# Attention and two gated layers in one kernel: five plain chunks and two units by seven products in the first layer, and attention placed every 13.5 gaps

## The chip, the cores and the metric

The kernel runs on one core of one Trainium2 chip. The metric is the device time of one execution in microseconds (us), the median of several. The engines of the core work side by side, each through its own list of instructions in program order: TensorE (PE in the profile, with its weight loads as PEld), VectorE (DVE), ScalarE (ACT), GpSimd (POOL) and SyncE (SP), which here issues nearly all transfers.

## The reference

Three stages, each fed by the one before, for 8 x 576 = 4608 tokens of 512 features.

```
kv  = einsum('bhsd,bhse->bhde', k, v)            # 8 batches, 8 heads, 576 tokens, 64 features
o   = einsum('bhsd,bhde->bhse', q, kv)
x   = o / sqrt(mean(o * o, -1) + 1e-6) * g_norm   # then laid out as 4608 x 512
x2  = ((x @ w1) * (x @ w2)) @ w3 @ w_out          # 512 -> 1024, 1024 -> 1024 -> 512
h   = x2 @ moe2_w_in                              # 512 -> 2048
out = (h * sigmoid(h)) @ moe2_w_out               # 2048 -> 512
```

All arrays are float32.

## The kernel before

**Precision.** Every large product runs in three passes: an operand is split into a high part (a cast to fp32r on ScalarE, `split`, L108) and a low part (a subtraction on VectorE), and TensorE adds high x high, high x low and low x high (`passes`, L112). Weights arrive as 64-bit words and are made into float32 on the chip by two ScalarE activations and one VectorE operation (`cv_scale`, `cv_bits`).

**Opening.** The list `ORDER` (L59) is written out by hand. It loads and splits w3 and the first layer's output weights, multiplies them into one matrix (`wch`, `wcl`), and computes attention for the first chunk of 512 tokens.

**First phase, plain chunks** (L791 to L844). There are nine chunks of 512 tokens. Those in `PLAIN` (L30: seven, all but 4 and 8) go through the first layer here. A chunk is 8 steps, and a step is three groups of 12 matmuls of 512 columns: `pa` and `pb` (the two input products) and, for the step before, the product with the combined matrix (`g2_mm`). Between the groups ScalarE copies `pa`, VectorE multiplies, and the result is split for the next step's third group. After the eighth step four output tiles are copied out of PSUM and written to DRAM (`x2d`).

Two other kinds of work are threaded between the groups:

- *Attention* of chunks 1 to 8. `event` (L664) puts each of its parts at a place counted in gaps; a gap is one group of 12 matmuls, and places are kept in half gaps. `att_step` (L694) emits what is due. For each chunk: k and v are loaded (`kv_load`, tiles 0 to 2 and later 3 and 4) and multiplied (`kv_mm`), the result is copied (`kv_out`); q is loaded (`q_load`, four tiles); two halves of `att_a` (TensorE) and `att_b` (four ScalarE operations); `att_c`, the row sums of squares on TensorE (L389); `att_d`, three ScalarE operations (L397 to L399); `att_e`, two VectorE operations; `att_h`, a ScalarE cast; `att_l`, a VectorE operation (L417); two halves of `att_r`, the matmuls that spread the scales (L427), and `att_x`, the VectorE products; and `att_f`, which splits the chunk into `xh`, `xl`, or, for a chunk that is not plain (`LATER`), writes it to DRAM (`xd`). The products of attention use two PSUM banks in turn. Chunk c + 1 is placed 20 gaps after chunk c (13 for the last).
- *Weights for the last phase* (`pieces`). `advance` (L295) takes the list one piece further: it writes the blocks that are ready to DRAM (`flush`), asks SP for the raw words three pieces ahead, and casts, scales, joins, sums and subtracts. The last phase needs each weight block in seven forms (the block's quarters and sums of them), each split. Sixteen blocks come from DRAM in three pieces each (`block`), twelve from weights that are on the chip already (`sum`). `ensure` calls `advance` twice a step, after the `pa` group and after the `pb` group.

**Last phase, seven products** (from L994). Units of `UNITS` (L32) hold twice as many tokens as the width given there. A unit is a list of blocks, and a block multiplies a 2 x 2 arrangement of quarters with seven products in place of eight; each product is 2 x 2 x 3 = 12 matmuls (`run`, L865). A unit "A" puts 1024 tokens that attention left in `xd` through the first layer in six blocks (a, b, a, b, out, out); a unit "B" puts tokens through the second layer in eight. Before a block, GpSimd forms sums of the operands (`sums`), and ScalarE and VectorE split them (`step`). After each product ScalarE copies or VectorE adds the result out of PSUM (classes `First`, `Second`, `Silu`, `Out`). The weights of each product (512 KB) are loaded by SP six products ahead in the stream, into the buffer that the product just run has left (`w_load`). The first block of a unit runs before the last block of the unit before.

## Time and profile before

| what | value |
|---|---|
| median of 3 runs | 1402.18 us (1401.04 to 1402.23) |
| the profiled execution, its own time | 1402.33 us |
| its span, first to last instruction | 1400.2 us |
| mean granted TensorE clock (share of 2.4 GHz) | 0.999 |
| busy share of PE, DVE, ACT, POOL | 99%, 59%, 46%, 21% |
| moved by DMA | 320.04 MB, mean 229 GB/s |

A busy share is an average over the whole span. What an engine costs is read from what TensorE waits for in each stage: the chain of waits tells that for the whole span, the time line for a few microseconds, and the table of stretches gives the busy time of each engine in a stage.

### The profile page before, as it was taken

Reading aid. Unit: us, or ns where it says so; the run is one execution under the profiler, and the core shown is the slowest. Engines: PE = TensorE matmul, PEld = TensorE weight load, DVE = VectorE, ACT = ScalarE, POOL = GpSimd, SP = SyncE. Lnnn points to the kernel's source line nnn. Section 1 sums busy time; section 2 is a strip of 40 time slices with the busy share of each in tenths; the row PEclk is TensorE's granted clock in tenths of the full one; section 3 lists DMA queues with packets and bytes.
Section 4 is the critical chain, followed back from the end, with each engine's and each line's share of the span. In section 5 each row is a group of like instructions: output and inputs, shape, how many; then the busy total and the mean of one; then the engine's idle time right before and its main releaser. Section 6 shows DMA issues by size and latency. Waiting matters only on the chain.

```text
span 1400.2 us, 19103 instructions
## 1 busy us (share of the span) xinstructions
PE 1386.7 (99%) x7084; PEld 1152.3 (82%) x7084; DVE 825.4 (59%) x1192; ACT 646.3 (46%) x1019; POOL 291.4 (21%) x190
## 2 busy tenths in 40 slices
PE   7999999999999999999999999999999999999998
PEld 4777787777877778888888888888888889999998
DVE  5856546464656663343764577455854576567458
ACT  5675535444453662323534354543534453543543
POOL 1000000000000002003522435124522352245222
PEclk9999999999999999999999999999999999999999
DMA  9754676769685747076687666866686668888886
GB/s 360 285 181 134 213 240 236 254 202 305 198 265 189 262 163 274 31 254 195 192 259 246 194 193 217 293 194 191 191 299 194 193 209 292 284 255 273 279 254 200
DMA packets 149868, 320.04 MB, mean 229 GB/s; under 512 B 14224, under 2 KB 72592, under 8 KB 149776
## 3 DMA queue, kind: packets, MB, share of 16 engines
q1 hardware_dynamic: 149200, 317.78, 69.3%
q8 instruction: 56, 0.92, 0.3%
q10 hardware_dynamic: 576, 1.05, 0.2%
q14 instruction: 36, 0.29, 0.1%
HBM read 246.42 MB, written 72.35 MB: 228 GB/s over the span
## 4 chain that ended last, share of the span: by engine, by line
PE 96%; DMA 2%; DVE 1%; ACT 0%; SPq 0%; issue 0%
PE ps L878 57%; PE x2ps L114 4%; PE pb L114 4%; PE pa L114 4%; PE x2ps L116 4%; PE x2ps L115 4%; PE pb L116 4%; PE pb L115 4%; PE pa L116 4%; PE pa L115 4%; PE wps L558 2%; PE kvps L338 1%; PE o L370 1%; DMA v<-v_l 1%; PE s L389 1%; DMA more_xl<-wo_l 1%
## 5 line engine op out<-in xcount | busy, mean ns | idle before, releaser
L878 PE MATMUL ps<-xo,w 128*128 128x512 f32 (+1 forms) x2016 | 424.6, 371 | 0.0
L878 PEld LDWEIGHTS ps<-xo,w 128*128 128x128 f32 x2016 | 369.0, 188 | 52.4
L878 PE MATMUL ps<-go,w 128*128 128x512 f32 (+1 forms) x1848 | 387.0, 369 | 0.4 <-issue 0.4
L878 PEld LDWEIGHTS ps<-go,w 128*128 128x128 f32 x1848 | 337.3, 188 | 46.7 <-issue 1.0
L778 DVE TENSOR_TENSOR go<-g,go 128x1024 fp32r<-128x1024 f32 (+1 forms) x110 | 124.9, 1137 | 113.7 <-ACT go L777 112.4
L888 DVE TENSOR_TENSOR c<-ps,c 128x512 f32<-128x512 f32 (+1 forms) x260 | 158.0, 636 | 55.1 <-PE ps L878 53.7
L765 POOL TENSOR_TENSOR x_t<-x2r 128x1024 f32<-128x1024 f32 (+1 forms) x12 | 26.9, 2239 | 543.8 <-DMA x2r<-xd 543.3
L777 ACT CAST go<-g 128x1024 fp32r<-128x1024 f32 (+1 forms) x110 | 104.8, 972 | 46.3 <-PE ps L878 45.1
L815 DVE TENSOR_TENSOR asb<-pb,asb 128x512 f32<-128x512 f32 x56 | 38.6, 690 | 125.4 <-PE pb L116 118.7
L765 POOL TENSOR_TENSOR g_t<-g 128x1024 f32<-128x1024 f32 (+1 forms) x44 | 100.7, 2290 | 49.2 <-DVE g L960 44.4
L765 POOL TENSOR_TENSOR g<-g,g_t 128x1024 f32<-128x1024 f32 (+1 forms) x22 | 48.4, 2198 | 261.4 <-DVE go L778 261.4
L109 ACT CAST ch<-asb 128x512 fp32r<-128x512 f32 x56 | 35.0, 624 | 118.9 <-DVE asb L815 118.7
L114 PE MATMUL pb<-xh,w12h 128*128 128x512 f32 x224 | 89.3, 399 | 0.3 <-ACT w12h L219 0.3
L114 PE MATMUL pa<-xh,w12h 128*128 128x512 f32 x224 | 89.3, 399 | 0.0
L114 PE MATMUL x2ps<-ch,wch 128*128 128x512 f32 x224 | 89.2, 398 | 0.0
L910 ACT COPY s<-ps 128x512 f32<-128x512 f32 (+1 forms) x40 | 21.7, 543 | 145.1 <-PE ps L878 145.1
L116 PE MATMUL pb<-xh,w12l 128*128 128x512 f32 x224 | 87.4, 390 | 0.6 <-DVE w12l L232 0.6
L778 DVE TENSOR_TENSOR go<-g_t,go 128x1024 fp32r<-128x1024 f32 (+1 forms) x44 | 75.4, 1713 | 20.6 <-ACT go L777 20.6
L115 PE MATMUL pb<-xl,w12h 128*128 128x512 f32 x224 | 87.4, 390 | 0.0
L116 PE MATMUL x2ps<-ch,wcl 128*128 128x512 f32 x224 | 87.3, 390 | 0.0
L116 PE MATMUL pa<-xh,w12l 128*128 128x512 f32 x224 | 87.3, 390 | 0.0
L115 PE MATMUL x2ps<-cl,wch 128*128 128x512 f32 x224 | 87.3, 390 | 0.0
(128 smaller groups left out, 1786.5 us busy)
## 6 DMA issues: line engine op xcount, KB each, us to landing
w<-wbd SPq DMA_DIRECT2D x322, 512.0 KB, 4.4
wbd<-bh SPq DMA_DIRECT2D x72, 256.0 KB, 3.2
raw<-wb_l SPq DMA_DIRECT2D x32, 512.0 KB, 5.3
wbd<-s SPq DMA_DIRECT2D x56, 256.0 KB, 3.2
q<-q_l SPq DMA_DIRECT2D x36, 256.0 KB, 4.6
k<-k_l SPq DMA_DIRECT2D x32, 256.0 KB, 4.9
v<-v_l SPq DMA_DIRECT2D x32, 256.0 KB, 5.1
raw<-w_l SPq DMA_DIRECT2D x14, 512.0 KB, 3.8
```

Of the source, the lines that this page charges most:

```text
L109: nc.scalar.copy(out=h, in_=x)
L114: nc.tensor.matmul(out=ps_out, lhsT=ah, rhs=bh, start=first, stop=False)
L115: nc.tensor.matmul(out=ps_out, lhsT=ah, rhs=bl, start=False, stop=False)
L116: nc.tensor.matmul(out=ps_out, lhsT=al, rhs=bh, start=False, stop=last)
L558: nc.tensor.matmul(out=wps[m], lhsT=(l if which == "lh" else h)[:, x:x + P], rhs=rhs, start=left[m] == all_of, stop=left[m] == 1)
L765: nc.gpsimd.tensor_tensor(out=x, in0=x if a == place else self.src[a], in1=x if b == place else self.src[b], op=ALU.subtract)
L777: nc.scalar.copy(out=t[:, 0, :, :self.w], in_=x)
L778: self.cuts[n].tensor_tensor(out=t[:, 1, :, :self.w], in0=x, in1=t[:, 0, :, :self.w].bitcast(F32), op=ALU.subtract)
L815: nc.vector.tensor_mul(out=asb, in0=pb, in1=asb)
L878: mm = lambda a, bb, start, stop: nc.tensor.matmul(out=o, lhsT=a, rhs=bb, start=start, stop=stop, skip_group_check=True)
L888: eng.tensor_tensor(out=out_, in0=a, in1=b, op=ALU.add)
L910: nc.scalar.copy(out=t[nm, d], in_=o)
```

## The change

Chunks 2 and 6 leave the plain form. With 4 and 8 they make two "A" units of 1024 tokens in the last phase. The attention parts get new places: chunk 2 begins at gap 10 and each next one 13.5 gaps later (the last one 4 gaps earlier than that), and the parts of one chunk stand closer. The pieces of the last phase's weights are taken at an even pace (`pace`, up to three calls a step) and the last four of the sixteen blocks are not among them: they are converted in the last phase (`late`, `late_all`), one step of their list at each product of certain blocks.

```
-PLAIN = (0, 1, 2, 3, 5, 6, 7)
+PLAIN = (0, 1, 3, 5, 7)
-UNITS = (("A", 512), ("B", 512), ("B", 512), ("B", 512), ("B", 384), ("B", 384))
+UNITS = (("A", 512), ("A", 512), ("B", 512), ("B", 512), ("B", 512), ("B", 384), ("B", 384))
+LRAW, LWH, LEVERY = 1, 3, 7
+LATES = (("a", 0), ("a", 1), ("out", 0))
+FIRST, PERIOD = 10, 13.5
+EARLY = 12
...
     for n in range(K2):
-        for role in range(3):
-            pieces.append((wb[2 * n + role] if role < 2 else None, "block", role, wbd[n // 2][:, :, n % 2]))
+        if n < EARLY:
+            for role in range(3):
+                pieces.append((wb[2 * n + role] if role < 2 else None, "block", role, wbd[n // 2][:, :, n % 2]))
...
-    gap = -6
+    at_ = dict(k=4, q=7, a=4.5, a2=2.5, c=8, d=8.5, e=9.5, r=10.5)
     for c in range(1, NCH):
+        gap = FIRST + PERIOD * (c - 2) - 4 * (c == B) if c > 1 else 1 - at_["a"]
         if 1 < c < B:
             event(gap, kv_mm, c, [0, 1, 2])
             event(gap, kv_load, c, [3, 4])
-            event(gap + 6, kv_mm, c, [3, 4])
-            event(gap + 6, kv_out, c)
+            event(gap + at_["k"], kv_mm, c, [3, 4])
+            event(gap + at_["k"], kv_out, c)
         if c + 1 < B:
-            event(max(gap + 6, 2), kv_load, c + 1, [0, 1, 2])
-        if c > 1:
+            event(max(gap + at_["k"], 2), kv_load, c + 1, [0, 1, 2])
+        if c + 1 < NCH:
             for p in range(KD):
-                event(gap_was + 11, q_load, c, p)
+                event(gap + at_["q"], q_load, c + 1, p)
         for i in range(2):
-            event(gap + 7 + 3 * i, att_a, c, i)
-            event(gap + 7 + 3 * i, att_b, c, i)
-        event(gap + 12, att_c, c)
-        event(gap + 13, att_d, c)
-        event(gap + 14, att_e, c)
-        event(gap + 14, att_h, c)
-        event(gap + 14, att_l, c)
+            event(gap + at_["a"] + at_["a2"] * i, att_a, c, i)
+            event(gap + at_["a"] + at_["a2"] * i, att_b, c, i)
+        event(gap + at_["c"], att_c, c)
+        event(gap + at_["d"], att_d, c)
+        for f in (att_e, att_h, att_l):
+            event(gap + at_["e"], f, c)
         for i in range(2):
-            event(gap + 17 + i, att_r, c, i)
-            event(gap + 17 + i, att_x, c, i)
-            event(gap + 17.5 + i + 1.5 * (c in LATER), att_f, c, i)
-        gap_was = gap
-        gap += 20 if c + 1 < B else 13
+            event(gap + at_["r"] + 2.5 * i, att_r, c, i)
+            event(gap + at_["r"] + 2.5 * i, att_x, c, i)
+            event(gap + at_["r"] + 2.5 + 2.5 * i + 0 * (c in LATER), att_f, c, i)
...
+    def pace(step, k):
+        all_ = 3 * (K1 * len(PLAIN) - 2 * K1 + 3)
+        if done < 2 * K1 - 1 + (len(pieces) - 2 * K1 + 2) * (3 * (step - K1) + k + 1) / all_ and done <= len(pieces):
+            advance()
...
             att_step(step, 0)
             if s_ == 0 and j + 1 < K1:
                 ensure(w12_piece.get(j + 1, 1) - 1)
-            elif not (lastc and j > 2):
-                ensure(done - 1)
+            else:
+                pace(step, 0)
...
             split(ch, cl, asb)
             ct[c, j] = ch, cl
+            if s_ > 0:
+                pace(step, 1)
             att_step(step, 3)
             if s_ == 0 and j + 1 < K1:
                 ensure(w12_piece.get(j + 1, 0))
-            elif not (lastc and j > 2):
-                ensure(done - 1)
+            else:
+                pace(step, 2)
...
+    lc = b_pool("lc")
+    def late(n):
+        dst = wbd[n // 2][:, :, n % 2]
+        def load(role):
+            t = lc.tile([P, 2 * N], U32, tag="raw", bufs=LRAW, name=f"lraw{n}_{role}")
+            nc.sync.dma_start(out=t, in_=wb[2 * n + role])
+            return t.rearrange("p (n two) -> p n two", two=2)
+        def scale(role, x):
...
+            nc.scalar.activation(out=t, in_=x[:, :, 1].bitcast(F32), func=AF.Prelu, scale=2.0 ** -112, alpha=-2.0 ** 32)
+            nc.scalar.activation(out=z, in_=x[:, :, 0], func=AF.Copy, scale=0.93 * 2.0 ** -29)
+            return t, z
...
+        raw = load(0)
+        yield
+        t0, z = scale(0, raw)
+        yield
+        raw = load(1)
+        bits(t0, z)
+        yield
+        yield
+        t1, z = scale(1, raw)
+        yield
+        bits(t1, z)
...
+        nc.vector.tensor_tensor(out=s1, in0=a21, in1=a22, op=ALU.add)
+        yield
+        nc.vector.tensor_tensor(out=s2, in0=s1, in1=a11, op=ALU.subtract)
+        nc.vector.tensor_tensor(out=s3, in0=a11, in1=a21, op=ALU.subtract)
+        nc.vector.tensor_tensor(out=s4, in0=a12, in1=s2, op=ALU.subtract)
+        x22 = high(a22)
+        yield
+        x1 = high(t1)
+        low(*x22)
+        low(*x1)
+        yield
+        write(A22, *x22)
+        write(A11, *x1)
+        x12 = high(s12)
+        low(*x12)
+        yield
+        x34 = high(s34)
+        low(*x34)
+        write(S1, *x12)
+        yield
+        write(S3, *x34)
+    def late_all():
+        todo = [late(n) for n in range(EARLY, K2)]
+        live = []
+        at0 = 0
+        while todo or live:
+            if todo and at0 % LEVERY == 0:
+                live.append(todo.pop(0))
+            at0 += 1
+            for x in list(live):
+                if next(x, 0) == 0:
+                    live.remove(x)
+            yield
+    lates, LATE = late_all(), None
...
         for n in range(7):
+            if (which, i) in LATES and next(lates, 0) == 0 and LATE is None:
+                LATE = b
             if first and n < 3:
                 ops.step(n + 4)
```

Here `bits`, `high`, `low` and `write` are one VectorE operation, one ScalarE cast, one VectorE subtraction and two transfers to DRAM.

## Rows read from the trace of the kernel before

**Rows 1.** The page: span, and part 1, busy time of each engine.

```profile
span 1400.2 us, 19103 instructions
...
PE 1386.7 (99%) x7084; PEld 1152.3 (82%) x7084; DVE 825.4 (59%) x1192; ACT 646.3 (46%) x1019; POOL 291.4 (21%) x190
```

**Rows 2.** The chain of waits: start us, length us, what.

```profile
180.51 1.55 PE kvps L338 x48
...
243.18 1.55 PE kvps L338 x48
...
591.60 783.48 PE ps L878 x3744
```

**Rows 3.** Time line of TensorE, first phase, first and last of 15 matmuls in a row.

```profile
239.62 0.39 PE L114 MATMUL x2ps<-ch,wch 128*128 128x512 f32 x1
...
242.79 0.39 PE L116 MATMUL pa<-xh,w12l 128*128 128x512 f32 x1
```

**Rows 4.** Line 935 (copy after a block's seventh product): durations ns, first and last start.

```profile
L935 ACT COPY g<-ps x4: 587/587/588, 609.3 to 648.8; 128x512 f32<-128x512 f32 x4
```

**Rows 5.** Time line, row sums and last scale operation of chunks 4, 5 and 6.

```profile
281.49 1.06 PE L389 MATMUL s<-sq,ones 128*32 128x512 f32 x8
...
290.30 0.75 DVE L417 SCALAR_TENSOR_TENSOR rhl<-u,low,rh 128x512 fp32r<-128x512 f32 x1 [0.69 <-ACT rh L413]
...
344.28 1.06 PE L389 MATMUL s<-sq,ones 128*32 128x512 f32 x8
...
353.83 0.75 DVE L417 SCALAR_TENSOR_TENSOR rhl<-u,low,rh 128x512 fp32r<-128x512 f32 x1 [0.69 <-ACT rh L413]
...
406.96 1.06 PE L389 MATMUL s<-sq,ones 128*32 128x512 f32 x8
...
414.10 0.75 DVE L417 SCALAR_TENSOR_TENSOR rhl<-u,low,rh 128x512 fp32r<-128x512 f32 x1 [0.69 <-ACT rh L413]
```

**Rows 6.** Stretches (us): length, busy of PE, PEld, DVE, ACT, POOL, PEclk, DMA share, GB/s.

```profile
118.00:540.00 422.00, 422.00 (x2394) 326.24 (x2391) 243.65 (x460) 202.71 (x374) 0.00 (x0) 1.00 0.68 224
305.97:368.65 62.68, 62.68 (x367) 48.64 (x368) 36.27 (x68) 29.41 (x55) 0.00 (x0) 1.00 0.73 239
270.00:280.00 10.00, 10.00 (x56) 7.71 (x55) 4.62 (x10) 5.75 (x11) 0.00 (x0) 1.00 1.00 360
667.70:686.80 19.10, 19.10 (x86) 15.83 (x85) 16.53 (x18) 10.64 (x14) 7.33 (x4) 1.00 0.61 194
686.80:705.80 19.00, 19.00 (x86) 15.73 (x85) 13.89 (x12) 11.14 (x16) 13.33 (x6) 1.00 0.63 193
```

**Rows 7.** Groups by line: names, shapes, count, busy us, mean ns, idle before.

```profile
L277 ACT CAST bh<-s 128x512 fp32r<-128x512 f32 x56 | 34.8, 624 | 2.7 <-DMA wbd<-bh 2.7
...
L205 DVE SCALAR_TENSOR_TENSOR t<-t,z 128x512 uint32<-128x512 uint32 x46 | 31.4, 684 | 0.0
L173 ACT ACTIVATE t<-raw 128x512 f32<-128x512 f32 x46 | 30.8, 670 | 10.0 <-DMA raw<-wb_l 6.4 <-DMA raw<-w_l 3.6
...
L247 DVE TENSOR_TENSOR s<-t 128x256 f32<-128x256 f32 x28 | 11.7, 420 | 0.0
```

**Rows 8.** DMA issues: queue, count, KB each, us from issue to landing.

```profile
w<-wbd SPq DMA_DIRECT2D x322, 512.0 KB, 4.4
...
raw<-wb_l SPq DMA_DIRECT2D x32, 512.0 KB, 5.3
...
k<-k_l SPq DMA_DIRECT2D x32, 256.0 KB, 4.9
```

**Rows 9.** Waits of SP's queue: line, waited for, us in total, times, longest us.

```profile
SPq L293 <- ACT bh L277: 78.3, 31, 5.8
```

**Rows 10.** Time lines of GpSimd and of VectorE, last phase.

```profile
666.38 2.39 POOL L765 TENSOR_TENSOR g<-g,g_t 128x1024 f32<-128x1024 f32 x1 [23.15 <-DVE go L778]
...
666.94 2.39 DVE L960 TENSOR_TENSOR g<-g,u 128x512 f32<-128x512 f32 x1
...
669.97 0.69 DVE L960 TENSOR_TENSOR g<-g,u 128x512 f32<-128x512 f32 x1
```

More of the change, by code (lines that the diff above doesn't have):

```diff
@@ L1000, in fused @@
         kind, w = UNITS[u]
+        assert kind == "A" or (which, i) in (("in", 0), ("in", 1)) or LATE is not None
         post = {"in": Silu, "a": First, "b": Second, "out": Out}[which](b, u, i)
```

19 lines of the change are left out of this document (added).

## The prediction

> **What bounds the kernel now.** I read the page first, then the chain of waits, then the time lines. The page says that TensorE is busy for 1386.7 of 1400.2 us [rows 1]: look for a price per matmul, and for waits that could appear, not for waits that could go. The chain of waits confirms it [rows 2]: from one attention part to the same part of the next chunk it is TensorE alone, and the whole last phase from 591.60 us is one piece of 783 us on TensorE. The other engines wait for TensorE, so what they do costs nothing until a queue of theirs makes TensorE wait.
>
> The price: in the first phase matmuls of 512 columns start at 239.62 us and so on to 242.79 us, 15 of them, 14 distances, so 0.2264 us each [rows 3]. In the last phase the copy that follows a block's seventh product runs first at 609.3 us and last at 648.8 us [rows 4]; the last one is two blocks and half a product (1.36 us) later, so a block of 84 matmuls takes (39.5 - 1.4) / 2 = 19.05 us, 0.2268 each. The form changes the count and not the price.
>
> **The change, part by part.** *Matmuls.* A plain chunk is 8 steps of 36, 288 matmuls for 512 tokens. A unit of 1024 tokens by seven products is 6 blocks of 84, 504. Two chunks go (576) and one unit comes (504): 72 fewer, 72 x 0.2266 = **-16.3 us**. All of it lies on the path. The attention of all nine chunks, the B units and the combined weight product keep their matmuls. Here a rule can be weighed. The rows say 0.227 us. The Trainium skill (TensorE: Matmul & The Clock Gate, Back-to-back issue gap) states about 131 ns for each matmul of 512 columns in a long stream; by that the sum would be an estimated -9.4 us. This trace doesn't agree at any place read, so the measurement decides and the rule gets no chance of its own.
>
> *Attention each 13.5 gaps, not 20.* A gap is 12 matmuls, 2.72 us. TensorE's own part for one chunk is the period, 62.67 us [rows 2], less 240 x 0.2264 = 54.3: 8.3 us, the same before and after. What shrinks is the room for the other engines. From the end of the row sums (att_c) to the matmul that spreads the scales (att_r) there were 5 gaps, 13.6 us. Now there are 2.5, which the grid rounds to 36 matmuls: 8.2 us. In that room ScalarE takes logarithm, exponential and square, VectorE two operations, ScalarE a cast, VectorE one more, all behind the chunk's own work and the conversions. Three chunks in a row stand at the three alignments that this order has [rows 5]. From the end of the sums (start plus 1.06) to the end of the last VectorE operation (start plus 0.75) they took 8.5, 9.2 and 6.8 us. Against 8.2 they are late by 0.3, 1.0 and 0: 0.45 each, x 8 chunks = **+3.6 us**, if the queues stay as they are. Bounds: 0, if the new places hit the short alignment; if 30% more conversions a step stretch the whole chain by 1.3 (11.1, 12.0, 8.9) it is 2.9 + 3.8 + 0.7, 2.5 each, +20 us. I take the measured lengths, since half to two thirds of the chain are its own seven operations, which don't grow.
>
> *Conversions.* Before, two pieces a step; now a pace of 70 pieces over 81 calls, 2.6 a step. For a period of 4.5 steps (162 matmuls, 36.7, plus 8.3: 45.0 us) I scale the row of 62.68 us [rows 6]. VectorE had 36.3 us there. A step's product, its low part and a share of the output copies are 2.25 operations at the 0.69 us of their kin [rows 7], 1.56 a step: 10.4; attention is 11 such, 7.6; the rest, 18.3, is 13.3 pieces of 1.37. After: 7.0 + 7.6 + 11.7 x 1.37 = 30.6 of 45.0, 68% where it was 58%. ScalarE by the same way goes from 29.4 of 62.7 to about 25 of 45. Neither is full: cost nothing, and the cover is each engine's spare third. If it is gone, the late instruction is the cast that the next second matmul group needs, a whole step ahead. A raw load gave ScalarE two half steps before; now two calls stand together behind the second group, so the shortest lead is one group, a product and a cast, 2.72 + 1.3 = 4.0 us, where a load takes 5.3 to land [rows 8]. ScalarE waited 6.4 us in all for such loads [rows 7]; more of this is likely, but hidden, as its next work for TensorE is 5 us off.
>
> *Transfers.* The period of 62.68 us moved 239 GB/s, 15.0 MB [rows 6]. Attention reads 8 pieces of 256 KB and 2 of 128 KB for k and v [rows 8] and 4 of 256 KB for q, 3.4 MB; outputs are 0.9; so a piece is 10.7 / 13.3 = 0.80 MB. After: 3.4 + 1.1 + 11.7 x 0.80 = 13.9 MB in 45.0 us, an estimated 308 GB/s. A stretch of 10 us shows 360 GB/s at a full share [rows 6]. So 86% of what was seen: cost nothing, with k and v the tightest. Their tiles 3 and 4 had 6 gaps, now 4 (10.9 us) against 4.9 to land. Bounds: 0, and 1 us a chunk if landing doubles and issuing takes 2 more.
>
> *SP.* It issues everything in program order and is often held by producers, 78.3 us for one ScalarE cast alone [rows 9]. The q loads of the next chunk now stand in the same place as this chunk's second half, whose tiles they take over, so SP is held there till TensorE passes; behind it stand raw loads and block writes, which have a call or more of lead. Nothing.
>
> *Four blocks of weights converted in the last phase.* Each takes two loads of 512 KB, four ScalarE activations at 0.67 us and four casts (2.7 + 2.3), ten VectorE operations (bits 2 x 0.68, sums 4 x 0.42, low parts about 2.5: 5.5 us) and eight writes [rows 7]; one every seven products, 19 us. The block of the first output half already has VectorE at 16.53 and ScalarE at 10.64 of 19.1 us, the next VectorE at 13.89 of 19.0 [rows 6]. 22.0 and 19.4 are over, by 2.9 and 0.4; operands are made three products (8.2 us) ahead, which hides it. The transfers of such a block are seven weight pieces of 512 KB, the two loads and 1.8 MB of writes, 6.5 MB in 19 us: 344 GB/s, just under the 360 seen; weights are asked for five products (13.6 us) ahead and land in 4.4 [rows 8], so 9 us of delay would be hidden. The second load waits on SP for ScalarE, a write for VectorE, each emitted a product earlier; the weight loads behind them have those same 9 us. Cost 0, bounds 0 and 3.3 (both blocks' excess, no lead).
>
> *Sum:* profiled execution 1402.33 (2.13 outside its span); -16.3 + 3.6 gives 1389.6. Its time is 0.15 above the median, so **1389.5 us**. Least: no stall, 1385.9.
>
> **Rivals.**
> 1. *The attention chain is stretched by the denser queues.* For it: VectorE goes to 68%, and the even chunks have their two VectorE operations behind a whole conversion call. Against it: the chain's own operations don't grow. At half the stretch (1.15: 9.8, 10.6, 7.8) lateness is 1.6, 2.4 and 0, 1.33 x 8 = 10.7 us: 1396.6.
> 2. *VectorE stands behind GpSimd in the last phase.* One VectorE addition of two SBUF tiles took 2.39 us where its kin take 0.69, beside a GpSimd subtraction from 666.38 to 668.77 [rows 10]. So each late VectorE operation may lose up to 1.7 us, at most one for each GpSimd operation. The output block and the one behind it have 4 and 6 of these [rows 6]. At half, the output block has 16.53 + 5.5 + 4 x 0.85 = 25.4 of 19.1, 6.3 over: 1395.8; it must eat the 8.2 us of lead first, which speaks against it. The Trainium skill (SBUF — State Buffer, Who interferes with whom) states that a VectorE instruction with two SBUF inputs and a GpSimd one that reads SBUF exclude each other for a whole instruction; the row of 2.39 us agrees.
> 3. *Slower: the pieces can't be made at the new pace*, with SP and the transfers as the place. 70 pieces must pass in 27 steps, 220 us, plus six attentions, 50: 3.86 us a piece, where the row of before has 62.67 / 13.3 = 4.7. If SP holds it at 4.2, the last chunk waits 24 us for the rest: 1410. It decides from 3.86 + 16.3 / 70 = 4.09 us on. For it: 308 GB/s asked. Against: SP mostly waits and TensorE was busy for all of the 422 us from 118 to 540 [rows 6].
>
> **How the numbers follow.** Forecast 0.63 (1385.9 to 1393.5, stalls from none to double), rival 1 0.15, rival 2 0.10, rival 3 0.08, and 0.04 for a mixture of losses that ends near 1402. A measurement of this kernel tells 0.2% (2.8 us) from no change. Faster: 0.63 + 0.15 + 0.10 = 0.88; same 0.04; slower 0.08. The range takes in the forecast and most of rivals 1 and 2: 1385.0 to 1399.0; below 1385.9 only for stalls of before that go.
>
> **What would show it.** Right: 7012 matmuls, distances still 0.2266 us, the last phase starting about 127 us earlier (two chunks of 65.2 us, less the stalls) and 114 us longer; TensorE waits only in front of the spreading matmuls, under 1 us each. Rival 1: longer waits there. Rival 2: TensorE waits in the first output block, after VectorE additions of 2.4 us. Rival 3: a long wait in the fifth chunk's third step, with DMA share at 1. I am wrong if matmul distances change, or if waits of TensorE in the first phase are none or over 8 us in sum.

## The result and the profile after

| | before | after |
|---|---|---|
| median | 1402.18 us | 1408.71 us (1407.77 to 1410.61, 5 runs) |
| the profiled execution, its span | 1402.33, 1400.2 us | 1409.83, 1408.0 us |
| the last phase begins | 591.60 us | 469.73 us |
| from there to the end of the span | 808.6 us | 938.3 us |

The ratio is 1.0052 (95% interval 1.0037 to 1.0066): slower by half a per cent, where 0.9% faster was forecast (1389.5 us). The page of the changed kernel, the lines that answer to [rows 1]:

```profile
span 1408.0 us, 19221 instructions
...
PE 1378.2 (98%) x7012; PEld 1141.2 (81%) x7012; DVE 883.3 (63%) x1227; ACT 659.7 (47%) x1032; POOL 329.1 (23%) x206
```

There are 72 fewer matmuls, as forecast. Their price has not changed either. Time line of TensorE in the first phase, as in [rows 3]:

```profile
252.89 0.39 PE L118 MATMUL pb<-xh,w12h 128*128 128x512 f32 x1
...
257.42 0.39 PE L120 MATMUL pa<-xh,w12l 128*128 128x512 f32 x1
```

These are 21 matmuls, 20 distances, 0.2265 us each. So the 16.3 us were won, and more than that was lost again. The chain of waits, as in [rows 2] (start us, length us, what):

```profile
469.73 40.84 PE ps L888 x180
...
511.47 5.48 DMA wbd<-lt
...
552.40 2.35 DMA wbd<-lt
...
585.36 6.07 DMA lraw<-wb_l
...
604.60 778.30 PE ps L888 x3720
```

Before, the last phase was one piece of TensorE work. Now its first 135 us are broken by transfers of the late blocks (`wbd<-lt`, a write; `lraw<-wb_l`, a raw load), and only from 604.60 us on is it one piece again. The two stages can be priced apart. Two plain chunks less are 576 x 0.2266 = 130.5 us, so without any stall the last phase would begin at 591.6 - 130.5 = 461.1: **8.6 us were lost in the first phase**. The same kernel without late conversions (e1 below) takes 922.8 us for the last phase: **15.5 us were lost there**. -16.3 + 8.6 + 15.5 = +7.8 us, the difference of the two spans.

Stretches of the changed kernel (us: length, busy PE, PEld, DVE, ACT, POOL, PEclk, DMA share, GB/s), as in [rows 6]:

```profile
90.00:470.00 380.00, 373.29 (x2164) 283.77 (x2163) 227.61 (x423) 191.23 (x349) 9.58 (x4) 1.00 0.74 247
...
507.80:527.00 19.20, 18.59 (x83) 15.04 (x82) 16.34 (x16) 7.39 (x14) 14.43 (x6) 1.00 0.93 311
...
565.00:605.00 40.00, 31.11 (x122) 24.46 (x122) 34.56 (x34) 21.97 (x33) 18.61 (x8) 0.91 0.65 214
580.00:590.00 10.00, 5.83 (x14) 4.57 (x15) 9.55 (x9) 5.57 (x9) 3.12 (x2) 0.67 0.82 225
180.00:190.00 10.00, 7.72 (x34) 5.93 (x34) 6.56 (x12) 4.61 (x8) 0.00 (x0) 1.00 0.97 318
190.00:200.00 10.00, 10.00 (x37) 7.63 (x37) 9.10 (x17) 5.68 (x10) 0.00 (x0) 0.83 0.67 215
```

TensorE was idle for 6.7 us between 90 and 470 us, and the 40 us from 565 are the worst of the last phase: 8.9 us idle while VectorE is busy for 34.6 of them. What TensorE waited for, first in the window from 90 to 470 us, then from 470 to 605 us (us in total, times, longest):

```profile
PE rb L431 <- DVE rhl L421: 4.0, 3, 2.3
PE kvps L342 <- DVE ob L438: 1.8, 2, 1.4
PE x2ps L118 <- DVE x2o L655: 0.9, 1, 0.9
...
PE ps L888 <- ACT u L943: 6.2, 2, 5.6
PE ps L888 <- DVE g L898: 2.7, 1, 2.7
PE ps L888 <- ACT c L991: 1.3, 1, 1.3
PE ps L888 <- issue: 0.6, 1, 0.6
```

In the kernel before there is no such row between 95 and 470 us at all. The first group is 6.7 us, the second 10.8. Most of the rest of the two losses is clock. The granted clock was 0.83 from 190 to 200 us and 0.67 from 580 to 590, so parts of these stretches ran at 1.2 GHz and not at 2.4. TensorE's time line behind its wait of 2.28 us for `rhl`:

```profile
189.31 0.50 PE L431 MATMUL rb<-rhl,spread 32*128 32x512 f32 x2 [2.28 <-DVE rhl L421]
...
191.48 0.63 PE L118 MATMUL x2ps<-ch,wch 128*128 128x512 f32 x1
...
193.61 0.63 PE L120 MATMUL x2ps<-ch,wcl 128*128 128x512 f32 x1
```

The last two are five distances apart, 0.426 us each where 0.2265 is usual. Some eight distances were so long: 1.6 us more for a wait of 2.3. From 565 to 605 us the granted clock was 0.91, and TensorE's 122 matmuls took 31.1 us where 122 x 0.2268 is 27.7.

TensorE's time line shows where the loss of the last phase lies:

```profile
567.56 11.04 PE L888 MATMUL ps<-xo,w 128*128 128x512 f32 x48
584.16 8.64 PE L888 MATMUL ps<-xo,w 128*128 128x512 f32 x24 [5.56 <-ACT u L943]
595.51 3.04 PE L888 MATMUL ps<-xo,w 128*128 128x512 f32 x12 [2.71 <-DVE g L898]
598.39 5.60 PE L888 MATMUL ps<-go,w 128*128 128x512 f32 x24
```

The 84 matmuls from 567.56 to 598.39 us are one block, the first of the second A unit. It took 30.8 us where a block took 19.05 before: 11.8 of the 15.5 us. The first output block, just before it, lost only some 1.8 (546.67 to 567.56 us).

ScalarE gives the direct reason for the longest of these waits. What it waited for from 470 to 605 us, at the line of the late blocks' first activation:

```profile
ACT lt L1021 <- DMA wbd<-lt: 16.0, 3, 6.5
ACT lt L1021 <- DMA lraw<-wb_l: 10.6, 3, 5.9
```

It stands for 16.0 us for the write that empties the buffer of the late block before, and for 10.6 us for raw words; the copies that TensorE needs (`u`, L943) stand behind it. The longest of the six, 6.5 us up to 580.01 us, is in its turn mostly VectorE's doing. The chain of waits there:

```profile
575.68 2.55 DVE lt L1035
578.24 1.66 DMA wbd<-lt
```

The write could only be issued at 578.24 us, behind a low part of the late block that took 2.55 us on VectorE.

### The profile page after: what moved, and what is told of

Its sections match the earlier page's. It is cut to its first block, busy times and chain, and to the rows that moved or that the text cites. A ratio compares the mean times of both kernels' runs of the same rounds, so it can differ in the third digit from the quotient of the medians.

```text
span 1408.0 us, 19221 instructions
## 1 busy us (share of the span) xinstructions
PE 1378.2 (98%) x7012; PEld 1141.2 (81%) x7012; DVE 883.3 (63%) x1227; ACT 659.7 (47%) x1032; POOL 329.1 (23%) x206
## 3 DMA queue, kind: packets, MB, share of 16 engines
q10 hardware_dynamic: 576, 1.05, 0.2%
## 4 chain that ended last, share of the span: by engine, by line
PE 89%; DMA 5%; DVE 3%; ACT 2%; issue 1%; SPq 1%; DVEq 0%; ACTq 0%
PE ps L888 62%; PE wps L562 3%; PE pb L118 3%; PE x2ps L118 2%; PE pa L118 2%; PE pb L120 2%; PE pb L119 2%; PE x2ps L120 2%; PE x2ps L119 2%; PE pa L120 2%; PE pa L119 2%; PE kvps L342 1%; PE o L374 1%; DMA wbd<-w12l 1%; DMA v<-v_l 1%
## 5 line engine op out<-in xcount | busy, mean ns | idle before, releaser
L888 PE MATMUL ps<-xo,w 128*128 128x512 f32 (+1 forms) x2352 | 504.9, 375 | 8.9 <-ACT u L943 6.2
L888 PEld LDWEIGHTS ps<-xo,w 128*128 128x128 f32 x2352 | 433.8, 189 | 76.6 <-ACT u L943 7.0
L888 PE MATMUL ps<-go,w 128*128 128x512 f32 (+1 forms) x2016 | 426.2, 371 | 2.3 <-ACT c L991 1.3
L888 PEld LDWEIGHTS ps<-go,w 128*128 128x128 f32 x2016 | 368.4, 188 | 56.4 <-issue 2.0
L823 DVE TENSOR_TENSOR asb<-pb,asb 128x512 f32<-128x512 f32 x40 | 27.6, 690 | 84.0 <-PE pb L120 66.7
L898 DVE TENSOR_TENSOR g<-ps,s 128x512 f32<-128x512 f32 (+1 forms) x48 | 30.1, 642 | 68.0 <-PE ps L888 62.0
L118 PE MATMUL pb<-xh,w12h 128*128 128x512 f32 x160 | 65.0, 406 | 0.0
L118 PE MATMUL pa<-xh,w12h 128*128 128x512 f32 x160 | 63.7, 398 | 0.0
L119 PE MATMUL x2ps<-cl,wch 128*128 128x512 f32 x160 | 63.0, 394 | 0.0
L120 PE MATMUL pb<-xh,w12l 128*128 128x512 f32 x160 | 62.5, 391 | 0.0
L119 PE MATMUL pb<-xl,w12h 128*128 128x512 f32 x160 | 62.4, 390 | 0.0
```

The source lines that it names most:

```text
L118: nc.tensor.matmul(out=ps_out, lhsT=ah, rhs=bh, start=first, stop=False)
L119: nc.tensor.matmul(out=ps_out, lhsT=ah, rhs=bl, start=False, stop=False)
L120: nc.tensor.matmul(out=ps_out, lhsT=al, rhs=bh, start=False, stop=last)
L823: nc.vector.tensor_mul(out=asb, in0=pb, in1=asb)
L888: mm = lambda a, bb, start, stop: nc.tensor.matmul(out=o, lhsT=a, rhs=bb, start=start, stop=stop, skip_group_check=True)
L898: eng.tensor_tensor(out=out_, in0=a, in1=b, op=ALU.add)
```

## The experiments

The theories, as the expectations name them. **S**: a late block has one buffer for each of its tiles (three for the casts and the scaled words), and ScalarE stands in program order until the write of the last block has left it. **V**: VectorE's late operations stand behind GpSimd's sums of the A units. **A**: the attention chain of the first phase, its length and its order on the engines, makes the stalls there. **D**: the density of the pieces and of their transfers does.

"Start" is where the last phase begins in the profiled execution, "rest" is from there to the end of the span. Both come from one execution, and the executions of a kernel spread by 1 to 9 us. In e1 the profiled one lies 2.0 us above the median, in e18 3.3; in e2 it lies 3.4 us below, in e13 3.2, in e12 2.7, in e15 1.7. So a price is given by the medians too where the two differ.

| run | median us | ratio to before, 95% | start | rest |
|---|---|---|---|---|
| after | 1408.71 | 1.0052 [1.0037, 1.0066] | 469.7 | 938.3 |
| e1 no late blocks | 1392.54 | 0.9933 [0.9917, 0.9950] | 469.9 | 922.8 |
| e2 late blocks every 10 steps | 1407.3 | 1.0043 [1.0029, 1.0057] | 471.2 | 930.9 |
| e5 late blocks without VectorE | 1398.54 (one run) | - | 467.6 | 929.1 |
| e8 late blocks without writes | 1402.71 | 1.0005 [0.9993, 1.0017] | 468.4 | 932.6 |
| e9 late blocks at other places | 1413.27 | 1.0081 [1.0063, 1.0098] | 468.8 | 942.8 |
| e13 no GpSimd sums in A units | 1402.89 | 1.0001 [0.9988, 1.0015] | 468.4 | 929.5 |
| e15 late blocks spread thinly | 1400.03 | 0.9986 [0.9977, 0.9996] | 468.4 | 928.2 |
| e4 e1 with 74 pieces | 1393.53 (one run) | - | 468.4 | 923.3 |
| e6 e1, scale earlier | 1393.29 | 0.9937 [0.9922, 0.9952] | 469.2 | 922.8 |
| e7 e1, outputs by GpSimd's queue | 1394.28 | 0.9941 [0.9924, 0.9958] | 469.1 | 922.9 |
| e10 e1, few block writes | 1392.29 | 0.9935 [0.9919, 0.9952] | 467.7 | 922.8 |
| e14 e1, more room at the end | 1396.21 | 0.9950 [0.9935, 0.9965] | 471.7 | 922.8 |
| e17 e1 with few pieces | 1385.82 | 0.9877 [0.9846, 0.9909] | 459.8 | 923.0 |
| e11 98 pieces, no late blocks | 1417.01 | 1.0111 [1.0095, 1.0127] | 493.9 | 922.9 |
| e12 92 pieces, two late blocks | 1413.79 | 1.0085 [1.0070, 1.0100] | 483.2 | 926.1 |
| e16 e15 and e14 | 1401.47 | 0.9990 [0.9980, 1.0001] | 471.3 | 927.4 |
| e18 e15, chain begun earlier | 1402.70 | 0.9993 [0.9977, 1.0008] | 472.5 | 931.7 |
| e19 e15, pieces kept out of the chain | 1418.66 | 1.0124 [1.0107, 1.0141] | 488.7 | 928.9 |

### The late blocks

**e1_no_late.** The late blocks are left out.

```
-    lates, LATE = late_all(), None
+    lates, LATE = iter(()), 0
```

> The change without the conversions in the last phase: the last two output blocks of each B unit read the weights of the first two, so four blocks of weights are never converted (left out). The last phase of the changed kernel took 934.9 us from 469.7 us on; by the matmul price it should take 919.5. Both theories of the last phase (ScalarE stands for transfers; VectorE stands behind GpSimd) expect the whole 15.4 us to go: 1393.3 us, the last phase 919 to 920 us, no wait of TensorE in it, the first phase unchanged (last phase starts at 469 to 471 us). If the loss were in the second A unit itself (its operands, its transfers) and not in the conversions: 1402 or more.

The rest is 922.8 us, in the chain of waits one piece of TensorE work from the start of the phase to 1367.6 us. The start is unchanged. So all of the late blocks' cost lies in the last phase, 15.5 us by the two profiles and 16.2 by the medians, and the change without it would be faster than the kernel before.

**e2_late_apart.** A late block every 10 steps.

```
-LRAW, LWH, LEVERY = 1, 3, 7
+LRAW, LWH, LEVERY = 1, 3, 10
```

> The late blocks begin every ten products, not every seven, so that one is nearly through its list when the next begins. Theory S (ScalarE stands for transfers): its waits for the writes that leave the single buffer (16.0 us) go, those for raw loads (10.6 us) stay; TensorE loses 3 to 8 us in the last phase, 1396 to 1401 us. Theory V (VectorE stands behind GpSimd and is full): the same VectorE work meets the same sums; TensorE loses 12 to 16 us, 1405 to 1409 us.

The waits for the writes that leave `lt` are gone, yet 8.1 us of the 15.5 stay in the profiled execution: ScalarE now waits 11.1 us for raw words and 7.3 us for the writes of another buffer (`lh`). By the medians 14.8 of 16.2 us stay, where theory S gave 3 to 8. S alone does not explain the loss.

**e5_no_late_vector.** The late blocks' ten VectorE operations are left out; loads, activations, casts and writes stay.

> The late conversions without their ten VectorE operations each (the words are not joined, no sums, no low parts: left out); the loads, the ScalarE operations and the writes stay in place. Theory S: the ScalarE waits stay near 16 and 10 us and TensorE loses 10 to 15 us in the last phase, 1404 to 1408 us. Theory V: no VectorE queue is left, TensorE loses 0 to 4 us, 1393 to 1397 us.

929.1 - 922.8 = 6.3 us are left, though ScalarE still waits 15.3 us for the same writes. So VectorE's part is some 9 us, by a single run.

**e8_no_late_writes.** The late blocks' writes are left out.

> The changed kernel with late conversions that don't write their results (left out; output blocks as in e1), so no buffer is held by a write and 7.3 MB less are moved; loads, ScalarE and all VectorE operations stay. If the two causes add up (VectorE 9.2 us by e5, writes 6.3): the last phase loses 8 to 10 us, 1400 to 1403 us. If the writes' waits are what lets VectorE fall behind at the wrong place: under 4 us, 1393 to 1396. If VectorE behind GpSimd is all of it: 13 us or more, 1405.

9.8 us are left, so the writes are worth 5.7. By the medians 10.2 are left and the writes are worth 6.0. Together with e5's 9.2 the 5.7 make 14.9 of 15.5: the two parts nearly add up.

**e9_late_off_gpsimd.** The same work in blocks that have fewer GpSimd sums beside them, the blocks `out 0` among them.

```
-LATES = (("a", 0), ("a", 1), ("out", 0))
+LATES = ((0, "a", 0), (0, "b", 1), (0, "out", 0), (1, "b", 1), (1, "out", 0))
```

> The late conversions complete, but in the blocks in which GpSimd forms few sums: a, the second b and the first out of the first A unit, the second b and first out of the second, in place of a, a, out, a, a. Theory V with exclusion as its cause (VectorE operations with two SBUF tiles wait out a GpSimd sum of 2.4 us): the stretched VectorE operations go and the loss in the last phase falls to 6 to 9 us, what the writes cost: 1398 to 1402 us. Theory V by load alone (5.5 us more in a block that is nearly full): the first output block is as full as before, loss 12 us or more, 1404 and up.

A miss of the theory that exclusion is all: 20 us lost in place of 15.5, as the theory of load had it (12 or more). TensorE now waits for VectorE itself (`v` 6.5, `xo` 3.1, `go` 2.7 us up to 750 us). The edit did part of what it was meant to do: VectorE's late operations took 31.1 us in sum, 44.2 in the changed kernel. But from 569 to 585 us five of them, and an operand split of 3.4 us, were still stretched among GpSimd's sums (the late one at 579.98 us took 2.62 us in place of 0.42). So less exclusion does not help where the work is packed into blocks in which VectorE has its own adds and operand splits to do; this run doesn't part the two.

**e13_no_gpsimd_sums.** The late blocks are complete; the GpSimd sums of the two A units are left out.

> The changed kernel with its late conversions, but GpSimd's operand sums in the two A units are left out (operands without them). VectorE's own number of operations is unchanged. V by exclusion (VectorE operations of two SBUF tiles wait for a GpSimd sum): the loss of the last phase falls from 15.5 to 4 to 8 us, about what e5 had without VectorE operations (6.3): 1397 to 1401 us. V by load alone: 11 us or more remain, 1404 and up.

6.7 us are left in the profiled execution, so GpSimd's sums are worth 8.8 of the 15.5; by the medians (10.4 left of 16.2) they are worth 5.8. That is more than half of VectorE's part. No row of VectorE or ScalarE waits for a result of GpSimd in the changed kernel from 470 to 605 us, so it is their running beside VectorE that counts, and not a wait for their results. The single operations show it. VectorE's time line of the changed kernel, low parts of a late block (`lt` two in one row, then `ls`):

```profile
508.48 3.74 DVE L1035 TENSOR_TENSOR lt<-lt,lh 128x256 fp32r<-128x256 f32 x2
512.14 2.88 DVE L1035 TENSOR_TENSOR ls<-ls,lh 128x512 fp32r<-128x512 f32 x1
```

GpSimd's time line of the same kernel at that time:

```profile
506.72 2.40 POOL L768 TENSOR_TENSOR g_t<-g 128x1024 f32<-128x1024 f32 x1 [44.08 <-DVE g L970]
509.20 2.47 POOL L768 TENSOR_TENSOR g<-g 128x1024 f32<-128x1024 f32 x1
511.75 2.72 POOL L768 TENSOR_TENSOR g_t<-g 128x1024 f32<-128x1024 f32 x1
```

VectorE's time line without the sums, the same operations (lines stand 6 further down):

```profile
507.10 1.02 DVE L1041 TENSOR_TENSOR lt<-lt,lh 128x256 fp32r<-128x256 f32 x2
510.35 0.69 DVE L1041 TENSOR_TENSOR ls<-ls,lh 128x512 fp32r<-128x512 f32 x1 [2.23 <-ACT lh L1037]
```

1.02 became 3.74 us and 0.69 became 2.88. Both rows end 0.55 us behind the end of a GpSimd sum (511.67 and 514.47 us). The rule of the Trainium skill that the prediction drew on (SBUF — State Buffer, Who interferes with whom) agrees with this.

**e15_late_spread.** Complete: a late block every 12 steps, in seven blocks, none of them `out 0`.

```
-LRAW, LWH, LEVERY = 1, 3, 7
-LATES = (("a", 0), ("a", 1), ("out", 0))
+LRAW, LWH, LEVERY = 1, 3, 12
+LATES = ((0, "a", 0), (0, "b", 0), (0, "b", 1), (1, "b", 0), (1, "b", 1), (2, "in", 0), (2, "in", 1))
```

> The changed kernel complete, its four late blocks begun every 12 steps in place of every 7, in seven blocks of the last phase (a0, b0, b1 of the first unit, b0, b1 of the second, the two first input blocks of the third) in place of six (a0, a1, out0 of the first two units): each block of weights leaves its single buffers before the next one begins, none lies in an out0 block, and two of the blocks have no GpSimd sums of an A unit beside them. If the loss of 15.5 us is density (buffers and exclusion in the same stretch), the last phase costs 922.8 plus 3 to 7: 1395.5 to 1400 us, faster than the kernel before (1402.2). If it is the amount of work, wherever it lies, the last phase still costs some 932 to 938 and the time is 1402 to 1409.

The loss falls from 15.5 to 928.2 - 922.8 = 5.4 us with the same work, by the medians from 16.2 to 7.5: more than half of it was density, not amount. VectorE's late operations took 23.3 us in sum where they had taken 44.2, so most of the exclusion is gone. The run spreads the work and also moves it out of the output blocks; it does not say what each is worth. What TensorE waits for from 468 to 750 us is a third of what it was; the three largest:

```profile
PE ps L888 <- ACT s L943: 1.9, 1, 1.9
PE ps L888 <- ACT v L920: 1.0, 1, 1.0
PE ps L888 <- DVE g L898: 0.3, 1, 0.3
```

This is the only complete version whose interval lies below 1, by 0.14%, less than the 0.2% that the prediction took as measurable. A second set of buffers for the late blocks was not tried.

### The stalls of the first phase

**e4_eight_blocks.** `EARLY = 8` on top of e1: four more blocks left out, 74 pieces in place of 86. (The list has 14 pieces for the first layer's weights, three for each of 12 blocks from DRAM and three for each of 12 from the chip; the expectations of e4, e11 and e19 count two fewer, and the prediction 70 in place of 72 for the even pace.)

> Only eight of the sixteen weight blocks are converted, all in the first phase, none in the last; the output blocks of the B units read the weights of the input blocks (left out: the conversion of eight blocks). Pieces to pass in the first phase: 72, not 84, with 12.6 MB of raw words becoming 8.4 and 14.7 MB less to write. Theory D (first phase held by transfers and buffers of the conversions): its loss falls from 8.6 us to under 4, the last phase starts at 463 to 466 us, 1387 to 1389 us. Theory A (attention parts too close, conversions beside the point): the loss stays at 7 to 9 us, start at 468 to 470, 1392 to 1394 us.

Start 468.4 in place of 469.9, but the one run's time lies 1.0 us above e1's median: a seventh fewer pieces show no gain clear of the spread, so the loss is not in proportion to their number. TensorE's waits are 7.2 us here, at partly other places (3.2 of them in front of a chunk's row sums).

**e6_scale_early.** On e1, `e = 9` in place of 9.5: the scale operations stand half a gap earlier.

> On top of e1 (no late conversions, 1392.5 us, last phase from 469.9 us on): att_e, att_h and att_l half a gap earlier (9, not 9.5), so that the even chunks' two VectorE operations stand ahead of the step's split and of a whole conversion call; the odd chunks' place on the engines' queues hardly changes. Theory A (the attention chain is too long for its 36 matmuls): TensorE's waits in front of the spreading matmuls fall from 3.9 to about 2 us, those of chunks 4 and 6 vanish, and with the clock that a wait costs 2 to 5 us are won: 1388 to 1391 us, last phase from 465 to 468. Theory D (transfers and the buffers of conversions hold VectorE, attention is only where it shows): within 1 us of 1392.5.

The waits for `rb` fall from 3.9 to 2.9 us, and a wait of 2.6 us for the output copies (`x2o`) comes instead. No gain.

**e7_outputs_by_gpsimd.** On e1, the writes of `x2o` are issued from GpSimd's queue and not from SP's.

> On top of e1: the plain chunks' output tiles are written to DRAM from GpSimd's queue, which is idle in the first phase, and not from SP's, where they stand behind conversion writes. Theory O (a chunk's fourth output copy waits on VectorE for the first one's write, and everything behind it on VectorE comes late: the stalls of TensorE follow the chunk ends at 160, 235 and 330 us): VectorE's wait for these writes falls from 7 to under 3 us, TensorE's loss of the first phase from 8.7 to 4 or less, 1388 us. Theory A: the waits for the writes go but the spreading matmuls wait as before, 1391 to 1393 us.

VectorE waits 9.7 us for these writes where it waited 7.0 in the changed kernel. SP's queue is not what delays them.

**e10_no_piece_writes.** On e1, only the first two blocks of weights are written in the first phase; the other writes are left out.

> On top of e1: only the first two weight blocks are written to DRAM in the first phase and the last phase reads them for every product (left out: some 40 MB of writes in the first phase); the conversions' arithmetic and loads stay, and attention stands where it stood. Theory D (the first phase is held by transfers: buffers of conversions, output tiles, k and v come late because the DMA share is near 1): VectorE's and ScalarE's waits for writes (8.0 + 7.9 + 6.9 us) go, the loss of the first phase falls from 8.7 to under 4 us, last phase from 463 to 465, 1387 to 1388 us. Theory A (the chain's own length and order): loss 7 or more, 1391 to 1393 us.

The start is 467.7, and TensorE waits 5.2 us where e1 has 6.3. By the medians it is 0.3 us faster than e1. So the load of these writes is not the cause of most of the stalls. The run says less than was meant, though: the write on which the first stall hangs belongs to the two blocks that were kept. The chain of waits of the changed kernel there:

```profile
161.84 4.10 DMA x2d<-x2o
...
166.06 0.70 DVE x2o L655
...
169.23 6.09 DMA wbd<-w12l
175.38 5.49 DMA wbd<-s
...
181.24 0.42 DVE s L254
...
188.42 0.76 DVE rhl L421
```

VectorE stands for an output write of the chunk before. Behind that write SP issues the pieces' writes (`wbd<-w12l`, then `wbd<-s`), so they land late, VectorE stands again until the last has left the buffer of the sums (`s`), and only then come the product, the cast and the seven scale operations of the attention chain. TensorE stands for their end.

**e11_all_early, e12_two_late.** `EARLY = 16` without late blocks (98 pieces), and `EARLY = 14` with two late blocks spread thinly (92 pieces); both complete.

> The change with all sixteen weight blocks converted in the first phase, 96 pieces at three calls a step, and none in the last phase (nothing left out). Last phase as in e1, 919 to 923 us. Theory D: 12 more pieces in the stretch that is already at a DMA share of 0.9 cost another 3 to 8 us there: 1396 to 1400 us. Theory A: conversions beside the point, 1393 to 1395 us. Either way faster than before if nothing waits for the last pieces.

> The change with fourteen blocks converted in the first phase and two in the last, one after the other, in the blocks a, b, second b of the first A unit and the first b of the second, where GpSimd has little to do and VectorE is half free (nothing left out). No buffer is asked for again before 20 us are over, so no wait for a write. Theory V (VectorE is what the late conversions overload): 0 to 3 us lost in the last phase, 1393 to 1397 us. Theory S with raw loads (ScalarE stands for a raw load ahead of a copy that TensorE needs): 3 us for each of four loads, 1402 and more.

Two misses: e11 was to take 1400 us at most, and e12's loss lies mostly in the first phase, where neither theory had put it. The start moves to 493.9 and 483.2 us. From 74 over 86, 92 and 98 pieces it is 468.4, 469.9, 483.2, 493.9: nearly flat, and above 86 some 2 us a piece. With 92 pieces ScalarE stands 27.6 us for raw words (14 times), with 98 it stands 10.6 us (7 times). The late blocks were cheaper than either place for them in the first phase.

**e14_more_room.** On e1, `att_r` a gap later, its halves closer; one gap more for the chain.

```
-r=10.5)
+r=11.5)
...
-            event(gap + at_["r"] + 2.5 * i, att_r, c, i)
+            event(gap + at_["r"] + 1.5 * i, att_r, c, i)
```

> The kernel without late conversions (e1: 1392.54 us, last phase starts at 469.90), in which the second scaling of the attention's output (att_r) begins one gap later (11.5 in place of 10.5 gaps into the period) and its halves follow each other by 1.5 gaps in place of 2.5; so the room of the chain from att_c to att_r grows from 2.5 to 3.5 gaps and the last step stays where it was. If the stalls are a chain whose room is too short, the waits of the tile rb (3.9 us in e1) go and nothing takes their place: last phase at 464 to 467, 1387 to 1390 us. If the period itself is what is too short (the engines' work of 13.5 gaps recurs in whichever step is moved), the wait turns up at the next key/value step or at the transposed loads, and the time stays within 1.5 us of 1392.5.

The waits for `rhl` fall to 1.7 us and 2.3 us come for the PSUM banks (`rb` behind `ob`); the start is 1.8 us later, the median 3.7 us above e1's. **e16_spread_and_room** put this into e15:

> e14 and e15 together, complete: the thin late blocks and the wider room of the attention chain. If the losses are separate, its time is e15's plus the difference of e14 to e1 (within 1.5 us).

1401.47 us: 1.4 more than e15, 0.7 less than the range that the expectation gives (1400.0 + 3.7, within 1.5). The wider room is of no use here either.

**e17_few_pieces.** e1 with 26 pieces in place of 86: nearly all conversions, raw loads and writes of the first phase are left out, and the last phase reads one block again and again.

> e1 with only 14 + 12 of its 84 + 14 pieces in the first phase: nearly all conversions, their raw loads and their writes are left out (the last phase reads the weights of the one block that is there, again and again). If the chain is stretched by the conversions in the queues of ScalarE and VectorE, the first phase ends at 461 to 463.5 us (461.1 without any stall) and the waits for rhl go. If the chain's own operations and its banks are too long for 13.5 gaps, it ends at 466 to 470 and the waits stay.

The start is 459.8 us, and between 90 and 460 us TensorE waits for nothing. By the medians the run is 6.7 us faster than e1. A stretch of it:

```profile
90.00:459.00 369.00, 369.00 (x2158) 281.11 (x2157) 138.93 (x217) 138.90 (x247) 9.93 (x4) 1.00 0.38 124
```

The chain without most conversions fits 13.5 gaps: theory A's length alone is out, and what stretches the chain are the conversions in front of it. The run leaves out their transfers with them; e10 had left out most of the writes alone and won 2.2 us at the start and 0.3 by the medians. Row sums and last scale operation of chunk 3, time lines of TensorE and VectorE in this run:

```profile
176.88 1.06 PE L393 MATMUL s<-sq,ones 128*32 128x512 f32 x8
...
182.45 0.75 DVE L421 SCALAR_TENSOR_TENSOR rhl<-u,low,rh 128x512 fp32r<-128x512 f32 x1 [0.69 <-ACT rh L417]
```

and in the changed kernel:

```profile
177.27 1.36 PE L393 MATMUL s<-sq,ones 128*32 128x512 f32 x8
...
188.42 0.75 DVE L421 SCALAR_TENSOR_TENSOR rhl<-u,low,rh 128x512 fp32r<-128x512 f32 x1 [0.68 <-ACT rh L417]
```

From the end of the sums to the end of the last scale operation it is 183.20 - 177.94 = 5.3 us alone and 189.17 - 178.63 = 10.5 us among the conversions; the room is 8.2. Chunk 3 shows the most. By the same two rows chunks 4, 5 and 6 took 9.1, 7.3 and 9.1 us in the changed kernel and 7.9, 5.3 and 7.9 in this run. So the chain's own length depends on its place in the steps: in the even chunks it fits by 0.3 us only. In the kernel before it took 8.5, 9.2 and 6.8 [rows 5].

**e18_chain_earlier.** e15 with `a2=2, c=7.5, d=8, e=9`: room at the front of the chain.

> e15 (the complete change with thinly spread late blocks, 1400.0 us) with the attention chain begun earlier at its front: the second pair of products (att_a) 2 gaps behind the first and not 2.5, the row sums and all up to the row factors half a gap earlier, att_r and what follows left in place. So the chain has 3 gaps of room and not 2.5, and the PSUM banks at its end come free when they did. If the room is what lacks, the waits for rhl (4.2 us) fall to under 1.5 and the first phase ends at 464 to 466.5 us, the whole at 1396 to 1398.5. If the wait only moves (to the products of the second pair, which then wait for their banks, or to kvps), it stays at 467.5 to 470.

A miss. The waits for `rhl` fall to 3.0 us, the output copies are waited for 3.5 us, and the start is at 472.5; the median is 2.7 us above e15's.

**e19_pieces_beside_chain.** e15 in which no piece is begun between a chunk's row sums and its spreading matmuls; a fourth call in each step makes up for it.

```
+        if any(a <= n < b for a, b in chains):
+            return
...
             att_step(step, 4)
+            if s_ > 0 and len(pieces) >= done and not (lastc and j >= 2):
+                pace(step, 3)
```

> e15 (complete, thinly spread late blocks: 1400.0 us, first phase to 468.4) in which no piece is begun between a chunk's row sums (att_c) and its spreading matmuls (att_r); a fourth call behind the second products of each step makes up for it, so all 84 pieces are made in the same 27 steps. If the place of the conversions in the queues stretches the chain, the waits for rhl (4.2 us) fall under 1 and the first phase ends at 461 to 465 us, the whole at 1393 to 1397. If it is their number in a period, the wait turns up elsewhere (at kvps, x2o, or pa and pb behind late products) and the first phase ends at 467 to 471, the whole at 1399 to 1403.

The largest miss: 20 us worse than e15 at the start, 18.6 by the medians. What TensorE waits for up to 495 us:

```profile
PE kvps L342 <- DVE ob L438: 9.9, 3, 6.1
...
PE rb L431 <- DVE rhl L421: 4.3, 2, 2.3
```

What ScalarE waits for from 90 to 490 us:

```profile
ACT t L177 <- DMA raw<-wb_l: 22.1, 10, 5.1
...
ACT bh L281 <- DMA wbd<-bh: 10.0, 6, 2.9
```

In e15 the two rows of ScalarE are 3.7 (3 times) and 7.9 us. Pieces that are taken closer together give their loads and writes less lead, so that ScalarE and VectorE stand inside a conversion, and whatever of the chain is behind it stands with them. The even pace that the change brought was the better one.

## Why the prediction was wrong, point by point

**Matmuls: right.** 7012, at 0.2265 us; -16.3 us. The 131 ns of the Trainium skill (TensorE: Matmul & The Clock Gate, Back-to-back issue gap) are seen in no stretch read here either.

**"Four blocks of weights converted in the last phase ... Cost 0, bounds 0 and 3.3": this step failed, by 15.5 us.** Three things were missing in it. First, the busy sums took VectorE's late operations at the durations that they have where GpSimd is idle; beside the sums the same ones took up to 2.9 in place of 0.69 us. e13 prices this at 8.8 us by its profile, 5.8 by the medians. This was rival 2, whose mechanism was right and whose price was 6.3 us; it was given 0.10 because three products of lead were to eat it first, and the lead did not. Its place was not right: it priced the first output block, where TensorE waited 1.3 us, and the forecast gave the block behind it an excess of 0.4 us; that block took 11.8 us too long. Second, the step followed the transfers to the loads behind them on SP, but not to ScalarE: a late block's first activation waits for the write that empties its only buffer, 16.0 us in all, and the copies of the running block stand behind it. e8 prices the writes at 5.7 us (6.0 by the medians). Third, the excess was reckoned block by block with the lead whole each time. A late block takes eleven steps and the next begins after seven, so two overlap; e15, where none do, shows that the same work costs 5.4 us (7.5 by the medians) when it is thin.

**"Conversions ... Neither is full: cost nothing, and the cover is each engine's spare third": this step failed too.** VectorE's busy share was forecast well enough: 68% for a period, measured 227.6 of 380 us, 60%. But from 90 to 470 us VectorE stood 14.1 us and ScalarE 10.9 us for transfers, and what was queued behind them stood too. Without most of the conversions the kernel is 6.7 us faster by the medians of e17 and e1, and the last phase begins at 459.8 in the profiled execution, with 461.1 worked out for no stall.

**Attention "+3.6 us, if the queues stay as they are": nearly right for its own waits, while the first phase lost 8.6 us.** The waits in front of the spreading matmuls are 4.0 us, and the room of 8.2 us was right. Their spread over the chunks was not: 0.3, 1.0 and 0 were forecast by alignment, and chunk 3 alone waited 2.3, chunks 4 and 6 0.9 each. So the sum is near by luck in part. What the forecast put at nothing is the rest: 2.7 us of waits for attention's banks and for the output copies, and 1.9 more, of which 1.6 is the clock behind chunk 3's wait. In chunks 3 to 6 the chain took 5.3 to 7.9 us with few conversions (e17) and 7.3 to 10.5 among them. That is the mechanism of rival 1; its price, 1.33 us for each chunk in front of the spreading matmuls, was not reached there (0.5).

**Transfers, SP: cost nothing, right as loads.** In stretches of 50 us from 150 to 400 us 266 to 314 GB/s were moved, 308 had been worked out, and leaving out most writes changed little (e10). SP's wait for casts fell from 78.3 us [rows 9] to 28.4:

```profile
SPq L297 <- ACT bh L281: 28.4, 16, 4.8
```

As single landings that an engine stands for they did cost: the write behind the first stall took 5.5 us.

**Rival 3 did not come.** The pieces kept pace, and no long wait stands in the fifth chunk's third step. With six pieces more the start moves by 13 us (e12), so the change stands close to an edge; but TensorE waits there at attention's parts, the last time at 419 us, and not at the end for the last pieces. With twelve more one wait of 3.6 us stands in the last chunk (e11).

**The forecast's chances.** Rivals 1 and 2 were priced one at a time, as alternatives. Both mechanisms came, one in each phase, and their 10.7 and 6.3 us alone would have made the sum about 0; with the single buffers' writes it is above. The prediction's own sign of being wrong, over 8 us of waits in the first phase, did not show (6.7); it had none for the last phase, where three quarters of the miss lie.

What is not settled: which single conversion call makes each of the later stalls of the first phase (232 to 249 and 321 to 342 us). Three ways of giving the chain room (e6, e14, e18) and one of clearing it (e19) moved the waits and removed none. Nor is it settled how much of the first phase's loss is the conversions' arithmetic in the queues and how much their transfers, since e17 leaves out both: the DMA share was 0.97 to 1.04 in the ten microseconds in which the three waits for `rhl` begin (180 to 190, 230 to 240, 320 to 330 us), but 1.05 from 250 to 260 us, where TensorE did not wait.

## What to carry to other kernels

Work that is put on an engine with a third of its time to spare is free only if it never stands: look, for each added operation, at what it waits for (the write that empties its buffer, the load that fills it, another engine's operation beside it), and at what the critical work behind it in program order then waits. Price it with the durations that the same operation has beside the work that will surround it, not with its mean. And when two rivals lie in different stages, add them; they are not alternatives.

## What was not expected of the hardware

- A VectorE subtraction of two tiles of 128 x 512 took 2.88 us beside GpSimd sums of 2.4 to 2.8 us, four times its 0.69. The same was paid by the operations around it: two of 128 x 256 just before took 3.74 us in place of 1.02, and the one at 520.21 us 2.89 in place of 0.68.
- After TensorE had stood for 2.3 of 10 us (180 to 190), it was granted 0.83 of its full clock in the next 10 us, though it was busy for all of them: part of that stretch was at 1.2 GHz, and matmuls there were 0.426 us apart. A wait of 2.28 us cost about 3.9. The waits of 0.3 to 1.4 us from 230 to 250 and from 320 to 350 us left the granted clock at 1.00.
- Above 86 pieces each further one cost 2 us of the first phase, while twelve fewer showed no clear gain: the edge is sharp, and nothing in the busy shares of VectorE and ScalarE (60% and 50%) shows where it lies.
